# One core, RWKV-6 attention and a squared-ReLU projection: a new written order of all engines, transfers and banks

## The chip, the core and the metric

The kernel runs on one core of a Trainium2 chip. The metric is the device time of one execution in microseconds. Before the change it is 180.9 us, the median of three runs (180.63 to 181.43).

## The reference

Two parts follow each other. The first is a linear attention with a decaying state, for 4 batches of 8 heads, 768 positions and 48 channels; the second is a projection to 2048 channels, a squared ReLU and a projection back to 384.

```python
for t in range(S):
    kt, vt, rt, wt = (k[:, :, t].copy(), v[:, :, t].copy(), r[:, :, t].copy(), w[:, :, t].copy())
    cur = np.einsum('bhd,bhe->bhde', u[None] * kt, vt)
    y[:, :, t] = np.einsum('bhd,bhde->bhe', rt, state + cur)
    state = wt[:, :, :, None] * state + np.einsum('bhd,bhe->bhde', kt, vt)
...
h = x @ w_in
r = np.maximum(h, 0.0)
g = r * r
return (g @ w_out).astype(np.float32)
```

## The kernel before, in words

The work is cut into 12 steps, three for each batch, of 256 positions (two chunks of 128). All steps are unrolled, and there is no loop on the chip. For step s the program has small operations, written as words like `rd_.9.0`: a name, the step, and an index.

- **Loads.** `ld.s.w`, `ld.s.k`, `ld.s.r` and `ld.s.v` (`load_step`, L178) fetch 384 KB each; `ld.g.i` and `ld.g.o` fetch a quarter of a weight matrix (768 KB, L188 and L194), and `cast` (L200) makes it bf16. All are issued by SP, one after the other, in the order of the list, together with the transposing transfers and the stores.
- **Decays.** `ww_` multiplies neighbouring decays (L264), `lw_` takes the logarithm on ScalarE, `cum_` sums it with matmuls (L324 to L328), `exp_` (L340) brings it back. `kw_` and `rw_` (L290, L286) fold a decay into k and r. `rd_.s.1` and `rd_.s.0` (L361, L358, VectorE) write the decayed keys and queries to `kdec_buf` and `rdec_buf`.
- **Attention.** For steps 0 to 3, TensorE transposes these (`tr_`, L374) and `rkt_` copies them to `kT` and `rT` (L391, L389). For steps 4 to 11 a transposing transfer does both (`dtr_`, L401 and L398). `p_` (L418) multiplies them in tiles of 64 rows, `pm_` masks (L432, L429), `su_` (L444, 64 rows) sums the new state, `ts_` and `sn_` (L454, L459) carry it on, `y_` (L481, 128 rows) and `yc_` (L491, 64 rows) make the output. The bonus of the position itself goes through `ku_`, `qp_`, `q_`, `qs_` and `vq_` (L297, L302, L307, L277, L316), and `ysb_` (L502) adds it.
- **Projection.** `yt_` and `xt_` (L514, L519), or from step 6 on a transposing transfer `dyt_` (L523), turn the output into `xT`. `m1_.s.g` (L534) is six matmuls of 128 by 256 into one of four banks, `rl_` (L543 on ScalarE, L545 on VectorE) takes the ReLU out of the bank, `sq_` squares, `m2_.s.c.q` (L562) is four matmuls of 128 by 384, and `os_` (L569, L571) and `store` (L575) bring the result out.
- **Warming.** `warm_.n.i` (L579) is n matmuls of 128 by 512 on zeros; their results are never read. They keep TensorE's clock up while the first loads are on the way.

What sets the order is `ORDER`, a list of 865 such words that was written by a search. The program walks through it once and issues each word as it stands, so that every engine's queue has the words of that engine in the list's order. `=A`, `=V` and `=G` say that ScalarE, VectorE or GpSimd does it, and `:0` and the like name the bank. Each engine works strictly in order: a word that waits holds up all words behind it on its engine. SP's queue is such a queue too.

Of the kernel before, what the change touches and what calls it, by code (L numbers as in the profile page):

```python
# [27 lines left out]
qp_.2=G pm_.2.1 pm_.2.0 su_.2:1 rl_.1.1=V ts_.2.0=V ld.2.i m1_.0.0:2 m1_.1.3:1 cast.i.2=A y_.2:1 q_.2 yc_.2.0
sn_.2.0 yc_.2.1 rl_.1.3=A m1_.0.5:3 ld.3.i m1_.1.5:1 ld.3.w m1_.0.4:0 rl_.0.0=A rl_.0.5=V qs_.2=A rl_.1.5=A
cast.i.3=G m1_.1.7:3 ld.0.o m1_.1.4:1 vq_.2=V ysb_.2=V rl_.0.4=A rl_.1.7=A ww_.3=G cast.o.0=G m1_.0.7:2 yt_.2:3  # L30
ld.2.o m1_.0.6:0 lw_.3 cast.o.2=G cum_.3:1 xt_.2=V rl_.0.7=V ld.3.o m1_.2.4:3 rl_.0.6=V sq_.0.1=A ld.1.o
sq_.0.0=A rl_.1.4=A m1_.2.2:2 sq_.0.2=A m1_.1.6:0 m1_.2.7:1 ld.3.r rl_.1.6=A sq_.1.1=A rl_.2.2=V rl_.2.4=V
# [5 lines left out]
p_.3.1:b ts_.3.0=A m2_.2.0.1:2 m2_.1.0.3 m2_.2.0.3 m2_.1.0.2 sq_.2.0=A ww_.4=G pm_.3.0 lw_.4 q_.3 qs_.3=A
cum_.4:0 m2_.2.0.0 ld.6.w v_.4=A pm_.3.1 ww_.5=G rw_.4=G sn_.3.0 ts_.3.1=V vq_.3=G ac_.4 al_.4 m2_.2.0.2
yc_.3.1:1 y_.3 m2_.2.1.0:1 m2_.2.1.2 os_.1.0=A kw_.4=V lw_.5 ysb_.3=V sn_.3.1 store.0.0 os_.2.0=A exp_.4 kw_.5=G  # L40
rd_.4.1 rd_.4.0 cum_.5:1 ac_.5 yt_.3:3 vs_.4.1=G xt_.3=A ld.5.r vs_.4.0=A al_.5 store.0.1 ld.6.r m2_.2.1.3
m2_.2.1.1 os_.2.1=V m1_.3.0:3 rl_.3.0=A exp_.5 su_.4:0 m1_.3.1:2 rl_.3.1=A m2_.1.1.3:0 m2_.1.1.1 dtr_.4.1
ku_.4=V qp_.4=V rw_.5=V m1_.3.7:2 rl_.3.7=A m1_.3.6:1 ts_.4.0=V dtr_.4.0 rl_.3.6=A m2_.1.1.2 m1_.3.5:3 rd_.5.1
rl_.3.5=A m1_.3.4:1 sn_.4.0 ts_.4.1=V p_.4.0:0 q_.4 rd_.5.0 qs_.4=A ww_.6=G vq_.4=G rw_.6=G p_.4.1:1 sq_.3.0=V
m2_.3.1.0:3 m2_.1.1.0 pm_.4.0 yc_.4.1:0 yc_.4.0 sq_.3.3=A m1_.3.3:2 rl_.3.4=A sq_.3.2=A pm_.4.1 y_.4 lw_.6
m1_.3.2:1 rl_.3.3=A rl_.3.2=A cum_.6:1 m2_.3.0.2:2 m2_.3.0.3 sq_.3.1=A m2_.3.1.3 m2_.3.1.1 ku_.5=G qp_.5=G
ld.5.v ysb_.4=V al_.6 ld.7.w ld.6.k ww_.7=G yt_.4:1 m2_.3.1.2 m2_.3.0.0 exp_.6 ac_.6 os_.1.1=V sn_.4.1 m2_.3.0.1
# [5 lines left out]
m2_.4.1.1:1 xt_.5=A qp_.6=G q_.6 qs_.6=G ld.7.k p_.6.0:1 ld.8.v yc_.6.1:0 ld.7.v ld.8.r p_.6.1:m store.1.1
ld.8.w vq_.6=G ku_.7=G pm_.6.1 sq_.4.3=A kw_.7=G m2_.4.1.0 m2_.4.1.2 m1_.5.1:0 rl_.5.1=A pm_.6.0 m2_.4.1.3
sn_.6.1 m1_.5.0:2 cum_.7:1 y_.6 m1_.5.7:3 vs_.7.0=A rl_.5.0=A os_.4.1=A ww_.9=V al_.7 m2_.4.0.0:0 rl_.5.7=V
m1_.5.2:2 m1_.5.6:1 ww_.8=G rw_.7=G exp_.7 ac_.7 m2_.4.0.1 vs_.7.1=G m2_.4.0.2 m1_.5.3:3 rl_.5.2=A sq_.5.0=A
v_.7=A rl_.5.3=A m1_.5.5:2 sq_.5.1=A ysb_.6=V vs_.8.0=G m2_.4.0.3 lw_.8 rl_.5.6=A rd_.7.1 qp_.7=V rd_.7.0
sq_.5.3=A su_.7:0 v_.8=G rl_.5.5=V rw_.8=V m1_.5.4:3 rl_.5.4=V m2_.5.1.0:2 cum_.8:1 sq_.5.2=A ts_.7.0=V al_.8
q_.7 m2_.5.1.1 m2_.5.1.3 store.1.0 ld.8.k ld.11.k ac_.8 store.3.1 dyt_.6 dtr_.7.1 dtr_.7.0 exp_.8 kw_.8=V
sn_.7.0 ts_.7.1=V m1_.6.2:3 m2_.5.1.2 m1_.6.3:1 ld.9.r ld.10.w sn_.7.1 os_.4.0=A rd_.8.1 m1_.6.1:0 os_.5.1=A  # L60
ku_.8=G m1_.6.7:2 rd_.8.0 rl_.6.2=V ld.9.k rl_.6.3=A qs_.7=A m1_.6.4:1 su_.8:1 rl_.6.7=A p_.7.1:m p_.7.0:0
qp_.8=G rl_.6.1=V ts_.8.0=V yc_.7.1:1 yc_.7.0 rl_.6.4=A sq_.6.1=A m2_.5.0.2:0 m1_.6.6:1 store.3.0 rl_.6.6=A
sq_.6.3=A dtr_.8.1 pm_.7.1 pm_.7.0 lw_.9 dtr_.8.0 m2_.5.0.1 m1_.6.5:2 y_.7 m1_.6.0:3 m2_.5.0.3 m2_.5.0.0
store.4.1 ku_.9=G q_.8 qs_.8=G ww_.10=G rl_.6.5=V vq_.7=V rl_.6.0=A vs_.8.1=A rw_.9=G sq_.6.0=A p_.8.0:m
p_.8.1:0 kw_.9=G qp_.9=G ysb_.7=V cum_.9:1 m2_.6.0.1:1 ld.9.v ld.10.k os_.5.0=A m2_.6.0.3 m2_.6.1.3:0 m2_.6.0.0
sq_.6.2=V m2_.6.0.2 m2_.6.1.0 sn_.8.0 al_.9 exp_.9 pm_.8.0 rd_.9.0 pm_.8.1 dyt_.7 v_.9=A ac_.9 m1_.7.7:2 y_.8:0
# [28 lines left out]
def kernel(  # L95
# [488 lines left out]
    def ld(n, x, h=None):  # L584
# [48 lines left out]
```

## Time and profile before

| what | value |
|---|---|
| median of the timed runs | 180.9 us (180.63 to 181.43) |
| span of the profiled execution | 178.8 us (no other time of this execution is given) |
| median less span | 2.1 us |
| PE (TensorE) busy | 171.0 us, 96% of the span |
| DVE (VectorE) busy | 138.0 us, 77% |
| ACT (ScalarE) busy | 133.4 us, 75% |
| POOL (GpSimd) busy | 108.0 us, 60% |
| transfers | 35.81 MB, mean 200 GB/s |

The span goes from the first to the last instruction of one profiled execution, and all durations below are from that execution. PEld is TensorE's weight load, which overlaps its matmuls. A busy matmul row includes its pipeline, so that rows that follow each other overlap; the distance from one start to the next tells what a matmul costs.

### The profile page before, as it was taken

The numbers are of one execution on the slowest core, as the hardware profiler recorded it, in microseconds if no ns is written. First come the engines' busy times: TensorE is split into PE (matmuls) and PEld (weight loads), VectorE is DVE, ScalarE is ACT, GpSimd is POOL, SyncE is SP. The second block draws the span as 40 slices with busy tenths as digits, with TensorE's granted clock in tenths as the row PEclk, the third lists the DMA queues.
The fourth block names the chain that finished last, engine by engine and source line by source line (L and its number), as shares of the span: only waits on it lengthen the run. The fifth ranks groups of instructions, "written<-read, shape, count | busy, mean of one in ns | idle before, by whom it ended". The sixth has DMA issues, their size and how long they took to land.

```text
span 178.8 us, 5697 instructions
## 1 busy us (share of the span) xinstructions
PE 171.0 (96%) x2383; PEld 123.9 (69%) x2385; DVE 138.0 (77%) x204; ACT 133.4 (75%) x238; POOL 108.0 (60%) x132
## 2 busy tenths in 40 slices
PE   7997889999999999999999999999999999999992
PEld 2354478888776677678677777788866779758761
DVE  5489998678999998998988999886678694705330
ACT  5287969999799768899889979779867528862601
POOL 6539986870784636998499788979997703000000
PEclk9999999999999999999999999999999999999999
DMA  5999999999999799979999998899927471402212
GB/s 144 268 263 252 259 346 361 344 368 260 266 243 237 191 216 185 290 166 259 273 291 151 213 255 224 222 175 245 226 79 148 55 48 40 127 12 88 88 44 88
DMA packets 78952, 35.81 MB, mean 200 GB/s; under 512 B 72144, under 2 KB 77392, under 8 KB 78928
## 3 DMA queue, kind: packets, MB, share of 16 engines
q1 hardware_dynamic: 78928, 35.46, 84.6%
q8 instruction: 18, 0.29, 0.7%
q14 instruction: 6, 0.05, 0.1%
HBM read 25.36 MB, written 4.72 MB: 168 GB/s over the span
## 4 chain that ended last, share of the span: by engine, by line
PE 56%; POOL 16%; DMA 10%; DVE 9%; issue 4%; SPq 3%; ACT 1%; POOLq 0%; ACTq 0%; DVEq 0%
PE m L562 16%; PE bk L534 11%; PE m L534 11%; PE bk L562 10%; DMA k_raw<-in_k_dram 7%; POOL ku L297 3%; DMA kT<-kdec_buf 3%; POOL r_raw L286 2%; SPq L178 2%; POOL ku L302 2%; DVE pmT L432 2%; PE att L418 2%; POOL ku L316 2%; POOL S L459 2%; DVE y_sb L502 2%
## 5 line engine op out<-in xcount | busy, mean ns | idle before, releaser
L534 PEld LDWEIGHTS <-wi_sb 128*128 128x128 bf16 x576 | 54.9, 98 | 10.7 <-ACT wi_sb L200 0.6
L562 PEld LDWEIGHTS <-gt 128*128 128x128 bf16 x384 | 36.7, 98 | 20.6
L534 PE MATMUL m<-xT,wi_sb 128*128 128x256 bf16 x306 | 40.2, 273 | 0.1
L551 ACT ACTIVATE gt<-gt 128x1024 bf16<-128x1024 f16 x37 | 38.1, 1051 | 0.5
L534 PE MATMUL bk<-xT,wi_sb 128*128 128x256 bf16 x270 | 35.8, 273 | 0.4 <-ACT wi_sb L200 0.4
L562 PE MATMUL bk<-wo_sb,gt 128*128 128x384 bf16 x192 | 35.6, 326 | 0.0
L562 PE MATMUL m<-wo_sb,gt 128*128 128x384 bf16 x192 | 35.0, 326 | 0.0
L543 ACT ACTIVATE gt<-m 128x512 f16<-128x512 f32 x33 | 19.4, 595 | 11.5 <-PE m L534 11.2
L543 ACT ACTIVATE gt<-bk 128x512 f16<-128x512 f32 x35 | 20.6, 596 | 7.2 <-PE bk L534 6.9
L545 DVE TENSOR_SCALAR gt<-m 128x512 f16<-128x512 f32 x18 | 12.3, 688 | 13.1 <-PE m L534 12.4
L432 DVE TENSOR_TENSOR pmT<-att,mask 128x1024 bf16<-128x1024 f32 x16 | 19.1, 1218 | 1.9 <-PE att L418 1.8
L316 POOL TENSOR_TENSOR ku<-v_sh,qs 128x768 f32<-128x768 bf16 x9 | 13.3, 1475 | 10.6 <-ACT qs L277 10.5
L459 POOL TENSOR_TENSOR S<-t_state,ac_buf 128x192 bf16<-128x192 f32 x20 | 12.2, 610 | 8.2 <-DVE t_state L454 5.5
L297 POOL TENSOR_TENSOR ku<-k_raw,u_bc 128x768 f32<-128x768 f32 x9 | 16.7, 1854 | 0.2 <-DMA k_raw<-in_k_dram 0.2
L502 DVE TENSOR_TENSOR y_sb<-att,ku 128x768 bf16<-128x768 f32 x12 | 11.5, 955 | 4.4 <-POOL ku L316 2.0
L290 POOL TENSOR_TENSOR k_raw<-k_raw,w_raw 128x384 f32<-128x384 f32 x8 | 8.1, 1012 | 10.9 <-DMA k_raw<-in_k_dram 10.9
L361 DVE TENSOR_TENSOR kdec_buf<-k_raw,att 128x768 bf16<-128x768 f32 x12 | 11.4, 950 | 3.7 <-ACT att L340 3.7
L277 ACT CAST v_sh<-v_raw 64x384 bf16<-64x384 f32 x26 | 13.2, 509 | 0.3
L302 POOL TENSOR_TENSOR ku<-ku,r_raw 128x768 f32<-128x768 f32 x7 | 12.7, 1811 | 0.2
L358 DVE TENSOR_TENSOR rdec_buf<-r_raw,att 128x384 bf16<-128x384 f32 x24 | 12.3, 547 | 0.6 <-POOL r_raw L286 0.4
L277 POOL CAST v_sh<-v_raw 64x384 bf16<-64x384 f32 x18 | 10.0, 556 | 3.3 <-DMA v_raw<-in_v_dram 2.0
L307 DVE TENSOR_REDUCE q<-ku 128x16 f32<-128x768 f32 x12 | 11.3, 944 | 0.0
(99 smaller groups left out, 250.6 us busy)
## 6 DMA issues: line engine op xcount, KB each, us to landing
w_raw<-in_w_dram SPq DMA_DIRECT2D x12, 384.0 KB, 5.7
k_raw<-in_k_dram SPq DMA_DIRECT2D x12, 384.0 KB, 6.2
r_raw<-in_r_dram SPq DMA_DIRECT2D x12, 384.0 KB, 5.6
v_raw<-in_v_dram SPq DMA_DIRECT2D x12, 384.0 KB, 6.7
out_dram<-o_sb SPq DMA_DIRECT2D x24, 192.0 KB, 4.2
w_st<-in_moe_w_in_dram SPq DMA_DIRECT2D x4, 768.0 KB, 8.9
w_st<-in_moe_w_out_dram SPq DMA_DIRECT2D x4, 768.0 KB, 8.3
u_bc<-in_u_dram SPq DMA_DIRECT2D x1, 192.0 KB, 5.0
```

What stands on the lines that cost most here:

```text
L277: copy(out[j * Q:(j + 1) * Q, c], src[c * Q:(c + 1) * Q, :, j])
L297: tensor_mul("ku_", s, h)(tiles["ku", s][:, hs], raw["k", s][:, hs, 1:3, :], u_bc[:, hs, None, :].to_broadcast([C, n, 2, D]))
L302: tensor_mul("qp_", s, h)(ku, ku, raw["r", s][:, heads(h), 0:2, :])
L316: tensor_mul("vq_", s)(vq[:], tiles["vs", s][:], tiles["qs", s][:, :, :, None].to_broadcast([C, 2, H, D]))
L358: nc.vector.tensor_mul(rdec[0][:, ps, j, :, 0:D], x[:, :, j, :].rearrange("p (a e) d -> p a e d", e=2), dec.rearrange("p (a e) d -> p a e ...
L432: nc.vector.tensor_mul(pmT, ps_p[:].rearrange("p e (x t) -> p (e x) t", t=C), mk.to_broadcast([C, 8, C]))
L459: nc.gpsimd.tensor_mul(t[:], tiles.pop(("ts", s, c))[:].rearrange("p (a d) -> p a d", a=HP), tiles["a_c", s][:, :, c, None].to_broadcast([ ...
L502: nc.vector.tensor_add(tiles["ysb", s][:, x].rearrange("p c (a e d) -> p (c a) e d", e=2, d=D), tiles["y", s][:, :, cols].rearrange("p e ( ...
L534: nc.tensor.matmul(ps1[:, j, :], wi_sb[:, n // 4, kk, n % 4 * 128:(n % 4 + 1) * 128], tiles["xT", s][:, :, kk, :], start=(kk == 0), stop=( ...
L543: nc.scalar.activation(rl, m1, AF.Relu, scale=RS)
L551: nc.scalar.activation(gt, rl, AF.Square)
L562: nc.tensor.matmul(m2, gt[:, 4 * q + n, c * C:(c + 1) * C], wo_sb[:, 4 * q + n, :], start=(summed[s, c] == 1 and n == 0), stop=(summed[s, ...
```

## The change

`ORDER` is written anew, again by a search, whose own picture of the machine now lets the fetching of instructions hold up the stream of loads. The list has 865 words as before, and the same ones, but for the warming, which is again nine words and 46 matmuls in other portions. Nearly every word stands elsewhere, 115 of them name another engine, and banks are handed out anew. `warm_` takes a third number that it doesn't use. Line numbers of functions are four lower after the change.

```diff
-ld.0.w ld.0.k ld.0.r ld.0.u ld.1.w ww_.0=V lw_.0 warm_.11.5 cum_.0:0 kw_.0=G exp_.0 rd_.0.1 ld.0.v warm_.8.5
+ld.0.w warm_.2.2.5 ld.0.k ld.0.r warm_.11.2.0 ld.0.u ld.1.w ww_.0=V ld.0.v lw_.0 ld.1.k kw_.0=V cum_.0:1 warm_.8.2.1
...
-    def warm_(n, i):
+    def warm_(n, i, x=0):
```

Ahead of `cum_.0`, TensorE had 11 warming matmuls; now it has 13 (2 and 11). Ahead of the first projection (`m1_`), both lists hold the same attention words on TensorE: steps 0 and 1 up to their outputs, the decays and the transposes of step 2. Counted along TensorE's queue, words of 64 rows (`p_`, `su_`, `yc_`) came in 25 unbroken runs, of which 20 stand behind the first `m1_`; now they come in 24, of which 18 stand behind it (the search counts 23, in its own way).

The first place is VectorE's queue at the program's start, behind the memsets. `ww` is the product of decays, `kdec_buf` and `rdec_buf` the decayed keys and queries, `ku` the bonus, `q` its sum, `rT` the transposed queries. Before:

```order
L264 TENSOR_TENSOR ww<-w_raw 128x384
L361 TENSOR_TENSOR kdec_buf_108<-k_raw,att_86 128x16x48
L358 TENSOR_TENSOR rdec_buf_107<-r_raw,att_86 128x4x2x48 x2
L264 TENSOR_TENSOR ww<-w_raw 128x384
L302 TENSOR_TENSOR ku<-ku,r_raw 128x768
L307 TENSOR_REDUCE q<-ku 128x16
```

And now:

```order
L260 TENSOR_TENSOR ww<-w_raw 128x384
L286 TENSOR_TENSOR k_raw<-k_raw,w_raw 128x8x48
L357 TENSOR_TENSOR kdec_buf_108<-k_raw,att_87 128x16x48
L354 TENSOR_TENSOR rdec_buf_107<-r_raw,att_87 128x4x2x48 x2
L293 TENSOR_TENSOR ku<-k_raw,u_bc 128x768
L385 COPY rT<-m_0_90 128x1024
L298 TENSOR_TENSOR ku<-ku,r_raw 128x768
```

VectorE takes over `kw_.0` (L286), the first product of the bonus (L293) and a copy of step 0's `rT` (L385); it gives `ww_.1` to GpSimd, the copy of step 1's `rT` to ScalarE, and `q_.0` moves back behind the masks.

The second place is SP's queue from the 10th load of k on. `xT` is a transposing transfer for the projection (step 7, and at the other end step 8), `rT` and `kT` those of step 9's queries and keys, `out_0_dram` a store. Before:

```order
L178 DMA v_raw_2392<-in_v_dram 128x8x96
L178 DMA k_raw_2394<-in_k_dram 128x8x96
L523 DMA_TRANSPOSE xT_2429<-y_sb_2381 128x6x128
L178 DMA v_raw_2532<-in_v_dram 128x8x96
L575 DMA out_0_dram<-o_sb_2142 128x384
L178 DMA w_raw_2592<-in_w_dram 128x8x96
L398 DMA_TRANSPOSE rT_2594<-rdec_buf1_109 128x8x128
L178 DMA r_raw_2603<-in_r_dram 128x8x96
L523 DMA_TRANSPOSE xT_2605<-y_sb_2536 128x6x128
L401 DMA_TRANSPOSE kT_2621<-kdec_buf1_110 128x8x128
```

And now:

```order
L174 DMA k_raw_2279<-in_k_dram 128x8x96
L571 DMA out_0_dram<-o_sb_2013 128x384
L519 DMA_TRANSPOSE xT_2371<-y_sb_2334 128x6x128
L174 DMA k_raw_2392<-in_k_dram 128x8x96
L174 DMA w_raw_2401<-in_w_dram 128x8x96
L397 DMA_TRANSPOSE kT_2445<-kdec_buf1_110 128x8x128
L174 DMA r_raw_2520<-in_r_dram 128x8x96
L394 DMA_TRANSPOSE rT_2529<-rdec_buf1_109 128x8x128
L174 DMA v_raw_2553<-in_v_dram 128x8x96
L519 DMA_TRANSPOSE xT_2559<-y_sb_2518 128x6x128
```

The load of step 10's v and the transfer of step 8's `xT` have moved behind step 9's two transposes. Of everything from the program's start, one load, one store and one `xT` fewer stand ahead of the later of these two.

More of the change, by code (lines that the diff above doesn't have):

```diff
@@ L28 @@
[L28 to L32, printed above, removed]
@@ L38 @@
[L38 to L42, printed above, removed]
@@ L43 @@
[L43 to L47, printed above, removed]
@@ L53 @@
[L53 to L57, printed above, removed]
@@ L58 @@
[L58 to L66, printed above, removed]
-yc_.8.1 rd_.9.1 su_.9:1 vs_.9.1=A yc_.8.0 rl_.7.7=A m1_.7.4:3 ld.10.v vq_.8=G ysb_.8=V m1_.7.0:2 lw_.10
@@ new lines @@
+rl_.4.2=A yc_.5.1 su_.6:0 ysb_.5=V m1_.4.3:2 ld.8.v ww_.7=G m1_.4.1:1 ku_.7=V ld.8.k rl_.4.3=A yt_.5:3 qs_.6=G
+m1_.4.6:0 xt_.5=A ld.8.r m1_.4.0:2 rl_.4.6=V rl_.4.1=A m1_.5.0:3 lw_.7 ts_.6.0=V sq_.4.3=V sq_.4.1=A store.1.1 sn_.6.0
+m1_.5.1:0 rl_.5.0=V m2_.4.1.2:1 v_.7=G rl_.4.0=A ts_.6.1=V ww_.8=V rl_.5.1=A p_.6.0:1 kw_.7=G p_.6.1:m sq_.4.0=A
+yc_.6.1:0 pm_.6.0 m2_.4.1.1 ld.9.w lw_.8 ld.9.v m2_.4.1.3 vq_.6=G pm_.6.1 v_.8=A m1_.5.5:0 sq_.5.0=A m1_.5.4:2 qp_.7=V
+vs_.7.0=G cum_.7:1 rl_.5.5=A y_.6 al_.7 m1_.5.3:3 ysb_.6=V exp_.7 m1_.5.2:0 ku_.8=G rl_.5.4=V dyt_.6 m2_.4.1.0
```

105 lines of the change are left out of this document (63 added, 42 removed).

## The prediction

> **What bounds the kernel now.** I began with the page: busy time, the slices, and the chain that ended last.
>
> ```profile
> span 178.8 us, 5697 instructions
> PE 171.0 (96%) x2383; PEld 123.9 (69%) x2385; DVE 138.0 (77%) x204; ACT 133.4 (75%) x238; POOL 108.0 (60%) x132
> ...
> DMA  5999999999999799979999998899927471402212
> ...
> PE 56%; POOL 16%; DMA 10%; DVE 9%; issue 4%; SPq 3%; ACT 1%; POOLq 0%; ACTq 0%; DVEq 0%
> ```
>
> TensorE (PE) is busy for 96%, and the transfers run at 9 tenths for 130 us. The next view splits the span where the first projection starts and where the last one ends; that start and that end follow, from TensorE's timeline and from the chain.
>
> ```profile
> 0.00:26.00 26.00, 21.98 (x324) 12.14 (x326) 20.53 (x36) 17.41 (x36) 19.30 (x30) 1.00 1.02 253
> 26.00:175.40 149.40, 148.98 (x2059) 111.71 (x2059) 117.45 (x169) 115.53 (x202) 88.68 (x103) 1.00 0.84 194
> 175.40:178.80 3.40, 0.01 (x1) 0.00 (x0) 0.00 (x0) 0.49 (x1) 0.00 (x0) 1.00 0.18 64
> ```
>
> ```profile
> 26.02 0.83 PE L534 MATMUL bk<-xT,wi_sb 128*128 128x256 bf16 x6 [0.39 <-ACT wi_sb L200]
> ```
>
> ```profile
> 37.37 0.66 PE m L534 x6
> ...
> 43.20 1.30 PE m L562 x8
> ...
> 173.46 1.96 PE bk L562 x12
> 175.50 0.49 ACT o_sb L569
> ```
>
> The first column behind the stretch is its length, the second PE's busy time. From 26.0 to 175.4 us PE is idle for 149.40 - 148.98 = 0.42 us, and a word of the projections follows the one before it every 0.65 us (0.66 for six of L534, 1.30 for two words of L562). So the time is made of three pieces: a head of 26.0 us until the first `m1_`, 149.4 us in which PE hardly waits, and 3.4 us behind it for the last copy and store. Busy PE time is not always work at full rate; what waits remain shows where the weight loads wait, in the waits of that engine from 26 us on (total, times, longest):
>
> ```profile
> PEld L418 <- issue: 1.4, 5, 0.3
> PEld L444 <- issue: 1.3, 5, 0.3
> PEld L491 <- issue: 0.8, 3, 0.3
> PEld L534 <- ACT wi_sb L200: 0.6, 1, 0.6
> PEld L491 <- DVE pmT L432: 0.5, 2, 0.3
> PEld L418 <- DMA kT<-kdec_buf: 0.4, 1, 0.4
> PEld L418 <- DVE kT L391: 0.3, 1, 0.3
> ```
>
> Those for named engines add up to 0.6 + 0.5 + 0.4 + 0.3 = 1.8 us. That is the most that a better order could take out of the middle; the three "issue" rows (13 waits, 3.5 us, so 0.27 each) stand in front of words of 64 rows.
>
> **The change, part by part.** The words are the same, so PE's work is the same. Ahead of the first `m1_` both lists put the same attention words on PE. What can differ is when the first `m1_` starts, how often PE changes between 64 and 128 rows behind it, and where PE waits. The median of 180.9 is 2.1 us over the profiled span of 178.8; I work on the span and add 2.1.
>
> *The head.* The rows are PE's timeline, then ScalarE's, GpSimd's and VectorE's at the program's start.
>
> ```profile
> 1.19 4.87 PE L579 MATMUL att<-warm 128*128 128x512 bf16 x11 [1.19 <-DVE half_ones L228]
> 5.86 0.28 PE L324 MATMUL att<-half_ones,lw_buf 128*128 128x2 bf16 x4
> ...
> 6.57 1.89 PE L579 MATMUL att<-warm 128*128 128x512 bf16 x8
> ```
>
> ```profile
> 6.78 0.80 ACT L340 ACTIVATE att<-att 128x768 f32<-128x768 f32 x1 [0.97 <-PE att L328]
> ...
> 24.50 1.47 ACT L200 CAST wi_sb<-w_st 128x1536 bf16<-128x1536 f32 x1 [1.57 <-DMA w_st<-in_moe_w_in_dram]
> ```
>
> ```profile
> 7.59 1.00 POOL L286 TENSOR_TENSOR r_raw<-r_raw,w_raw 128x384 f32<-128x384 f32 x1 [0.34 <-DMA r_raw<-in_r_dram]
> ```
>
> ```profile
> 7.66 0.95 DVE L361 TENSOR_TENSOR kdec_buf<-k_raw,att 128x768 bf16<-128x768 f32 x1 [2.47 <-ACT att L340]
> ...
> 9.99 0.80 DVE L264 TENSOR_TENSOR ww<-w_raw 128x384 f32<-128x384 f32 x1 [0.45 <-DMA w_raw<-in_w_dram]
> 10.71 0.95 DVE L302 TENSOR_TENSOR ku<-ku,r_raw 128x768 f32<-128x768 f32 x1
> ...
> 18.22 0.68 DVE L389 COPY rT<-bk 128x1024 bf16<-128x1024 bf16 x1
> ...
> 24.93 0.55 DVE L519 COPY xT<-bk 128x768 bf16<-128x768 bf16 x1
> ```
>
> Eleven warming matmuls take from 1.19 to 5.86, 0.42 each, and the decay sum `cum_.0` (L324) starts as they end. The order has 13 there now. Two more cost 0.85 at this rate, or 0.47 at that of the eight later ones (1.89 / 8 = 0.24). `cum_.0` moves by 0.5 to 0.85, and with it the exponential at 6.78 and VectorE's start at 7.66. A page of the Trainium skill, "TensorE: Matmul & The Clock Gate" (section "Part 1: The HAM clock gate (the "warmup" mystery)"), says that the array runs at half rate until about 3.4 us of activity have gone by; by it the two would come after the release and cost the smaller figure. The trace has the slow rate for at least 4.7 us, so the rows decide here.
>
> From 7.66 to 25.48 (24.93 + 0.55) VectorE (DVE) has one long wait, 0.45 at `ww_.1`, which is GpSimd's now; in its place stands a product that waits for nothing new. In the same stretch it gains the bonus product (0.95, as L302 of that shape) and step 0's copy (0.68), and loses `ww_.1` (0.80) and step 1's copy (0.68): +0.15. So `xT` of step 0 is later by (0.5 to 0.85) - 0.45 + 0.15 = 0.2 to 0.55 us, at 25.7 to 26.0. The first `m1_` needs also its weights' cast, which ends at 24.50 + 1.47 = 25.97 since the load lands then; the same bytes are queued ahead of this load as before, so I leave it there. The later start of the two is thus 26.0, and the transposes that PE does just ahead of it can add some tenths: +0.2, with 0 and +0.85 (nothing absorbed) as ends.
>
> *Changes between 64 and 128 rows.* Behind the first `m1_` there are 18 runs of 64-row words instead of 20. Their price is between 0.1 us (a word of `m1_` takes 0.76 instead of 0.66 behind a run, in the rows below) and twice that with the wait of 0.27 in front: 0.1 to 0.37 for a run. I take 0.2: -0.4 (-0.2 to -0.7).
>
> ```profile
> 33.62 0.37 PE att L491 x32
> 33.99 0.76 PE m L534 x6
> ```
>
> *Waits that go.* The 0.42 us of idle PE belong to the old order: -0.4 (0 to -1.8, the sum of the weight loads' waits above).
>
> *Waits that come.* PE reaches the attention of late steps earlier. Six words of the projections that stood ahead of `p_.9.0` stand behind it now (two of L562, four of L534): 6 x 0.65 = 3.9 us. Before, this word waited for its transposed keys, as the chain shows, and the transfers around it moved this:
>
> ```profile
> 119.72 5.12 DMA kT<-kdec_buf
> 124.88 0.65 PE att L418 x32
> ```
>
> ```profile
> 110.00:120.00 10.00, 10.00 (x179) 7.37 (x179) 8.89 (x15) 7.91 (x15) 8.68 (x12) 1.00 0.97 179
> 120.00:130.00 10.00, 9.78 (x166) 7.99 (x164) 7.12 (x11) 9.02 (x16) 9.45 (x10) 1.00 1.14 240
> ```
>
> The keys landed at 124.84, so the margin was nil. PE now wants them at 124.88 - 3.9 - 0.4 (runs) - 0.4 (idle) + 0.2 (head) = 120.4. Ahead of the later of step 9's two transposes stand one load (0.39 MB), one store and one `xT` (0.20 MB each) fewer: 0.79 MB at 240 GB/s (the last column) is 3.3 us, so they land at 121.5 if the stream is as dense as before. That is 1.1 us late. Where the old queue stood still while SP waited (179 GB/s from 110 to 120 against 240 after it: a quarter of 10 us), the stream can be up to 2.5 us earlier, and nobody waits. Between 0 and +1.1 I take the middle, +0.6. `xT` of step 8 comes just behind in SP's queue, and an `m1_` just behind on PE; its lateness is the same one, not a second. On SP, everything behind a transpose that waits for VectorE waits too, and that is where a further delay would come from.
>
> The fetches of instructions, which the search took into account, are in the page as a queue of their own:
>
> ```profile
> q8 instruction: 18, 0.29, 0.7%
> ```
>
> 0.7% of 16 engines' 178.8 us is 20 us, or 1.1 us of one transfer engine for each of the 18. A transfer spread over 16 engines lands with its slowest, so each fetch may hold up the stream by up to 1.1 us; I cannot see where they fall now, and this is why the term above isn't nil. The Trainium skill's page "Runtime: NRT & Kernel Launch" (section "Instruction fetch mechanics") speaks against planning for them: it calls the cost of crossing a 16 KiB block mostly hidden. By it the term of +0.6 would shrink to nothing, and the sum would be 180.3.
>
> *The end.* PE's last word is an `m2_` in both lists, behind it one copy and one store: 3.4 us as before, since the store of the other half is issued during PE's last words. The other engines are busy for 60 to 77% of the span, and the 115 words that changed hands go in all directions: I cost this at nothing, under the cover of PE's 96%; without it, it would show as waits in the middle, which the term above holds.
>
> Sum: 178.8 + 0.2 - 0.4 - 0.4 + 0.6 = 178.8; with 2.1 it is 180.9. For the few tenths between terms I see no sign.
>
> **The rivals.** *No wait at all (faster).* If the transfers come in time, the list runs PE without a pause behind the head. Then 180.9 - 0.6 (the term of waits that come) leaves 180.3, and if half of the weight loads' other waits (1.8 - 0.4) go too, 179.6. For it: only 0.42 us were idle before, so a list can do it. Against: that leaves no more than about 1.3 us to gain in all, and PE reaches its late words earlier than before with the same transfers.
>
> *The stream is late at step 9 (slower).* Place: `p_.9.0`, whose transposes must land by 120.4. If a fetch or a waiting transpose holds SP's queue for another 1.1 us on top of the 1.1 late above, PE stands for 2.2 us, and since PE has no slack behind it, all of it stays: 180.9 - 0.6 + 2.2 = 182.5. It decides from a landing at 121.9 on (1.5 late, 181.8). For it: the slices of the transfers at 9 tenths until 130 us, and a margin of nil at this very word. Against: the old queue had quiet stretches.
>
> *The head in full (slower).* If VectorE absorbs nothing of the 0.85 and the keys are 1.1 late as well, 180.9 + 0.65 + 0.5 = 182.0. That the new order does not reach the engines is no rival: their queues differ as shown.
>
> **How the numbers follow.** A difference of 0.5% (0.9 us) is about what a measurement of this kernel can tell from none; the three runs before lie within 0.8 us. My forecast, no change at 180.9, has 0.5. No wait at all ends below 180.0 in its further half, and I give what lies there 0.22. The late stream has 0.2 and the full head 0.08, both above 181.8. So: faster 0.22, the same 0.50, slower 0.28. Leaving 0.1 out at each side, the range goes from 179.7 (near the end of the first rival) to 182.7 (just over the second).
>
> **What would show it.** In the profile after: the first L530 row of PE between 25.9 and 26.6 us (the head); PE's idle time from there to its last product under 1.5 us; "issue" waits of 64-row words fewer by about two; at step 9's first L414 word a wait for a transposing transfer of 0 to 1.1 us; 3.4 us behind the last product. I'm wrong if PE has several waits of over 0.5 us behind the head, for loads or for GpSimd (then the order hangs on something that I took as covered), or if the first projection starts before 25.5 us (then the head had a slack that I did not see).

## The result and the profile after

The changed kernel takes 189.75 us (median of four runs, 188.5 to 191.08), the old one on the same chip 181.09: the ratio is 1.0485, 95% interval [1.043, 1.0541]. The forecast was no change, 179.7 to 182.7. The kernel is slower, and the time lies far above the range and above each of the rivals, of which the highest was 182.5. All ratios below are against runs of the old kernel on the same chip in the same batch (medians 180.25 to 181.39). A ratio leaves out runs that took over 1.5% longer than the fastest of their kernel; the medians count every run.

The page of the changed kernel, the lines that answer to those of before, and the granted clock, which was 9 in every slice before:

```profile
span 189.3 us, 5690 instructions
...
PE 174.3 (92%) x2382; PEld 126.3 (67%) x2385; DVE 144.5 (76%) x207; ACT 129.3 (68%) x230; POOL 113.7 (60%) x138
...
PEclk9999957999999999999999999999999999999999
DMA  6999899999996149999999999999949124000214
...
PE 58%; DVE 16%; DMA 10%; POOL 8%; issue 3%; ACT 2%; SPq 1%; DVEq 0%; POOLq 0%; ACTq 0%
```

The operations are the same, yet VectorE is busy for 6.5 us more and GpSimd for 5.7 us more (ScalarE for 4.1 us less). An estimate tells longer instructions from words that changed hands: if every instruction of the two profiles is charged at a short duration of its own form (the tenth percentile), what goes beyond that grows from 6.6 to 12.7 us on VectorE and from 7.3 to 12.6 on GpSimd, and hardly on ScalarE (3.0 to 3.2). So nearly the whole increase is instructions that took longer. TensorE's clock is halved in the sixth slice and lowered in the seventh, and the transfers have a hole in the 13th to 15th. VectorE's share of the chain has grown from 9 to 16%. The same three pieces as before, from the first `m1_` to the last product:

```profile
0.00:28.43 28.43, 22.93 (x323) 13.62 (x327) 22.70 (x37) 18.22 (x37) 19.46 (x29) 0.92 1.02 260
28.43:185.90 157.47, 151.32 (x2061) 112.71 (x2059) 121.80 (x171) 110.59 (x192) 94.19 (x109) 0.99 0.80 176
185.90:189.30 3.40, 0.08 (x1) 0.00 (x0) 0.00 (x0) 0.49 (x1) 0.00 (x0) 1.00 0.52 186
```

The head is 28.43 - 26.02 = 2.41 us longer, the middle 157.47 - 149.40 = 8.07, and the tail has not changed: together the 10.5 us between the spans. The profiled execution is the one of 191.08 us, so this is 1.8 us more than lies between the medians. Of the middle's 8.07, TensorE's idle time makes 6.15 - 0.42 = 5.73 (157.47 - 151.32 against 149.40 - 148.98); the other 2.34 is counted as busy, being matmuls at the half clock or behind a late weight load.

**The head.** TensorE's timeline, with two places where it stands still just before the projections, and the first `m1_`:

```profile
22.60 0.24 PE L320 MATMUL att<-half_ones,lw_buf 128*128 128x2 bf16 x4 [1.74 <-DVE pmT L428]
...
24.66 0.42 PE L487 MATMUL att<-S,rT 64*64 64x48 bf16 x16 [1.48 <-DVE y_sb L498]
...
28.43 1.49 PE L530 MATMUL m<-xT,wi_sb 128*128 128x256 bf16 x6
```

The same stretch in windows of 1 us; the last three columns are the granted clock, the transfers' share and GB/s:

```profile
24.00:25.00 1.00, 0.34 (x16) 0.29 (x15) 1.00 (x2) 0.93 (x6) 0.86 (x1) 0.54 1.03 356
...
30.00:31.00 1.00, 1.00 (x7) 0.74 (x6) 1.00 (x1) 0.00 (x0) 1.00 (x2) 0.55 1.14 319
31.00:32.00 1.00, 1.00 (x40) 0.81 (x39) 0.88 (x2) 0.85 (x2) 1.00 (x1) 1.00 1.30 284
```

A mean of 0.54 between 24 and 25 us and of 0.55 between 30 and 31 puts the half clock at about 24.1 to 30.9 us, 6.8 us long, and from 24.66 on TensorE has all the work there is. Six matmuls of `m1_` follow each other in 1.28 us there (1.49 to the end of the last) instead of 0.66. In the old kernel six warming matmuls stood ahead of `cum_.2` and four behind it, in just these two holes (one of the six has no record):

```profile
19.77 1.24 PE L579 MATMUL bk<-warm 128*128 128x512 bf16 x5 [0.16 <-issue]
...
21.38 1.02 PE L579 MATMUL bk<-warm 128*128 128x512 bf16 x4
```

**The middle.** TensorE's waits from 28 us on (total, times, longest):

```profile
PE m L414 <- ACT gt L539: 1.2, 1, 1.2
PE att L414 <- DMA kT<-kdec_buf: 1.2, 1, 1.2
PE bk L558 <- DVE wo_sb L196: 1.1, 1, 1.1
PE m L558 <- DVE gt L541: 0.7, 1, 0.7
PE m L510 <- DVE y_sb L498: 0.5, 1, 0.5
```

Four of these are the several waits of over 0.5 us that the prediction named as what would prove it wrong, though it named loads and GpSimd, and the rows name ScalarE, VectorE and a transposing transfer. They stand, in order of the rows, at `p_.9.1`, `p_.6.0`, `m2_.0.1.2`, `m2_.1.0.2` and `yt_.4`. Two causes show behind them. The first is VectorE's timeline ahead of the two `m2_` words:

```profile
44.96 1.82 DVE L549 TENSOR_TENSOR gt<-gt 128x1024 bf16<-128x1024 f16 x1
46.70 2.21 DVE L298 TENSOR_TENSOR ku<-ku,r_raw 128x768 f32<-128x768 f32 x1
48.84 1.17 DVE L282 TENSOR_TENSOR r_raw<-r_raw,w_raw 128x384 f32<-128x384 f32 x1
49.94 1.26 DVE L196 CAST wo_sb<-w_st 128x1536 bf16<-128x1536 f32 x1
```

GpSimd works without a pause beside these four. Before, such a square took 0.69 us, with GpSimd idle until 45.08:

```profile
44.54 0.69 DVE L553 TENSOR_TENSOR gt<-gt 128x1024 bf16<-128x1024 f16 x1
```

The old product of L302, of the second row's shape, took 0.95. The second cause is SP's queue in the changed kernel (start, duration of the issue):

```profile
52.83 2.99 SPq L174 DMA_DIRECT2D k_raw<-in_k_dram  x2
63.25 0.36 SPq L571 DMA_DIRECT2D out_dram<-o_sb  x1
67.78 1.33 SPq L394 DMA_TRANSPOSE rT<-rdec_buf  x1
...
70.53 0.58 SPq L174 DMA_DIRECT2D w_raw<-in_w_dram  x1
```

`store.0.0` waits from 55.82 to 63.25 for ScalarE's copy, the transpose behind it until 67.78 for VectorE, and three loads that wait for nothing stand behind both. That is the hole in the transfers. TensorE is busy all the while; the price comes later. The chain of waits runs through the load and through the engines behind it to a word of TensorE:

```profile
70.53 5.47 DMA w_raw<-in_w_dram
...
79.58 0.97 DVE y_sb L498
80.59 0.51 PE m L510 x6
```

### The profile page after: what moved, and what is told of

It reads as the page before. It is cut to its first block, busy times and chain, and to the rows that moved or that the text cites. A ratio compares the mean times of both kernels' runs of the same rounds, so it can differ in the third digit from the quotient of the medians.

```text
span 189.3 us, 5690 instructions
## 1 busy us (share of the span) xinstructions
PE 174.3 (92%) x2382; PEld 126.3 (67%) x2385; DVE 144.5 (76%) x207; ACT 129.3 (68%) x230; POOL 113.7 (60%) x138
## 4 chain that ended last, share of the span: by engine, by line
PE 58%; DVE 16%; DMA 10%; POOL 8%; issue 3%; ACT 2%; SPq 1%; DVEq 0%; POOLq 0%; ACTq 0%
PE m L558 15%; PE bk L530 11%; PE bk L558 9%; PE m L530 9%; DMA w_raw<-in_w_dram 6%; DMA kT<-kdec_buf 3%; PE m L575 3%; DVE ku L298 2%; DVE rdec_buf L354 2%; POOL ku L293 2%; PE att L414 2%; DVE y_sb L498 2%; DVE gt L549 2%; PE att L477 2%; POOL ww L260 1%
## 5 line engine op out<-in xcount | busy, mean ns | idle before, releaser
L558 PEld LDWEIGHTS <-gt 128*128 128x128 bf16 x384 | 36.2, 98 | 22.2 <-issue 2.4
L530 PE MATMUL bk<-xT,wi_sb 128*128 128x256 bf16 x300 | 40.2, 276 | 0.7 <-DVE xT L515 0.3
L530 PE MATMUL m<-xT,wi_sb 128*128 128x256 bf16 x276 | 37.0, 276 | 0.0
L547 ACT ACTIVATE gt<-gt 128x1024 bf16<-128x1024 f16 x33 | 34.3, 1053 | 0.2
L539 ACT ACTIVATE gt<-m 128x512 f16<-128x512 f32 x36 | 21.0, 596 | 10.1 <-PE m L530 9.8
L549 DVE TENSOR_TENSOR gt<-gt 128x1024 bf16<-128x1024 f16 x15 | 13.4, 895 | 3.8 <-ACT gt L539 3.8
L293 POOL TENSOR_TENSOR ku<-k_raw,u_bc 128x768 f32<-128x768 f32 x8 | 15.1, 1892 | 0.4 <-DMA k_raw<-in_k_dram 0.3
L541 DVE TENSOR_SCALAR gt<-bk 128x512 f16<-128x512 f32 x17 | 11.6, 684 | 3.1 <-PE bk L530 3.1
L286 POOL TENSOR_TENSOR k_raw<-k_raw,w_raw 128x384 f32<-128x384 f32 x10 | 11.3, 1128 | 2.9 <-DMA w_raw<-in_w_dram 2.3
L336 ACT ACTIVATE att<-att 128x768 f32<-128x768 f32 x12 | 9.6, 801 | 4.0 <-PE att L324 1.7
L273 POOL CAST v_sh<-v_raw 64x384 bf16<-64x384 f32 x20 | 11.7, 584 | 0.8
```

What stands on the lines that cost most here:

```text
L273: copy(out[j * Q:(j + 1) * Q, c], src[c * Q:(c + 1) * Q, :, j])
L293: tensor_mul("ku_", s, h)(tiles["ku", s][:, hs], raw["k", s][:, hs, 1:3, :], u_bc[:, hs, None, :].to_broadcast([C, n, 2, D]))
L530: nc.tensor.matmul(ps1[:, j, :], wi_sb[:, n // 4, kk, n % 4 * 128:(n % 4 + 1) * 128], tiles["xT", s][:, :, kk, :], start=(kk == 0), stop=( ...
L539: nc.scalar.activation(rl, m1, AF.Relu, scale=RS)
L547: nc.scalar.activation(gt, rl, AF.Square)
L549: nc.vector.tensor_mul(gt, rl, rl)
```

## The experiments

My theory was that three things add up: the clock that falls in the two holes, VectorE and GpSimd slowing each other, and SP's queue standing still. The rival was that one of them carries it all, the others following from it.

| kernel | median us | ratio to the old kernel, 95% interval |
|---|---|---|
| changed | 189.75 | 1.0485 [1.043, 1.0541] |
| `head_before` | 185.44 | 1.0254 [1.0186, 1.0322] |
| `head_after` | 183.36 | 1.0153 [1.0109, 1.0198] |
| `fill` | 185.06 | 1.0278 [1.0206, 1.0351] |
| `sq_act` | 188.46 | 1.0372 [1.0302, 1.0443] |
| `cold_before` | 181.71 | 1.008 [1.0044, 1.0115] |
| `fill_loads` | 184.47 | 1.0189 [1.01, 1.0278] |
| `fill_loads_r` | 183.61 | 1.0149 [1.0079, 1.0219] |
| `mended` | 183.79 | 1.0173 [1.0095, 1.0252] |
| `mended_head` | 182.96 | 1.0142 [1.0065, 1.022] |
| `loads_r` | 186.09 | 1.0215 [1.0158, 1.0272] |
| `warm13` | 180.87 | 0.9994 [0.9967, 1.002] |

**Head and rest apart.** `head_before` has the old order, engines and warming up to the first projection, and the new order from there on; `head_after` is the reverse, with three banks renamed.

```diff
 head_before: words ahead of the first m1_ as in the old order, the rest as in the new
 head_after:  words ahead of the first m1_ as in the new order, the rest as in the old
+yt_.0:1 tr_.2.1:2 tr_.2.0:0
```

> The words that the new list has ahead of its first projection, in the old list's order, on its engines and with its warming; behind them the new list unchanged. In the profile after, TensorE's last product stands 12.1 us behind the sum of its products with the old head: 2.4 us of that when the first projection starts, 1.2 us more because its first two words run at half clock, 8.5 us in waits behind. Theory 'the head alone': the later waits follow from the late head, so nearly all goes, 181 to 182 us. Theory 'each part its own': the head's 3.6 us go and the later waits stay, 185.5 to 186.5 us. Rival 'the head does not matter': the later waits are set by the transfers, and take up what the head gives back, 189 us.

> The reverse: the words that the old list has ahead of its first projection, in the new order, on the new engines and with the new warming (three of them in other banks than the new list gives them, so that no bank is taken while it is in use); behind them the old list unchanged. Theory 'each part its own': 181 + 3.6 = 184.5 us, give or take 0.7, with a clock that falls to half near 24 us. Theory 'the head alone': over 187 us. Rival 'the head does not matter': 181 us.

Either part alone is slower than the old kernel, by 2.5% and by 1.5%; together they would be 4.1%, and the whole is 4.85%. So head and rest each carry a part, the rest the larger. `head_before` ends at the lower edge of what was expected of two separate parts (185.5 to 186.5), `head_after` 0.4 us under it (183.8 to 185.2). In the profile of `head_before` the clock stays full and the first `m1_` starts at 26.49, yet the middle takes 154.59 us, 5.2 more than the old one's: that much of the 8.07 is there without the new head.

**The two holes.** `fill` is the new order with 28 matmuls of 256 columns on zeros, into columns that nothing reads, in the two places.

```diff
-p_.1.0:1 ld.2.v
+p_.1.0:1 fill_.15 ld.2.v
...
-cum_.2:1 kw_.2=G
+cum_.2:1 fill_.13 kw_.2=G
```

> The new list with 28 more matmuls of 128 by 256 on zeros, in columns of a bank that nothing else uses then: 15 behind the product of step 1's keys and queries, where TensorE idled from 20.9 to 22.6 us, and 13 behind the decay sum of step 2, where it idled from 23.2 to 24.7. Theory 'clock': the granted clock stays at 1.0 from 24 to 31 us, the first two projection words follow each other in 0.66 us instead of 1.28, and the first starts near 27.2 instead of 28.4: 1.5 to 2.5 us less, 187.3 to 188.3 us, if the later waits do not take it up. Rival 'the clock falls whatever the idle time': 189.7 us and the same half clock.

The median falls by 4.7 us, the ratio by 2.1 points, and the two intervals are apart. That is more than I expected. Its clock and its first `m1_`:

```profile
PEclk9999999999999999999999999999999999999999
```

```profile
25.58 0.83 PE L530 MATMUL m<-xT,wi_sb 128*128 128x256 bf16 x6
```

The projections start 28.43 - 25.58 = 2.85 us earlier, ahead of the old kernel's 26.02. Not all of that is the holes: the warming at the program's start took 4.29 us in this execution and 5.73 in the profile of the changed kernel (see the end). `fill_loads`, of which below, has the holes filled and as slow a start (its `cum_.0` at 6.63, that of the changed kernel at 6.70), and its first `m1_` starts at 26.72; so at the same start the holes account for 1.7 us. A second effect shows too. GpSimd's casts at 42.9 to 48.1 us, which had stood beside VectorE's products without a pause, now wait for their loads, since the engines come there earlier and the loads do not; VectorE runs alone in the gaps, and the waits at the two `m2_` words (1.1 and 0.7 us) are gone from the list of waits. So in the changed kernel the late head had set the two engines against each other.

`cold_before` puts the question to the old kernel, where it takes the ten matmuls out of the two holes and changes nothing else.

```diff
-p_.1.0:m warm_.6.1 vq_.0=G
+p_.1.0:m vq_.0=G
...
-vs_.1.1=A pm_.1.0 qs_.1=A exp_.2 warm_.4.1 su_.1:m
+vs_.1.1=A pm_.1.0 qs_.1=A exp_.2 su_.1:m
```

> The old order without its two late warming words, the six matmuls behind p_.1.0 and the four behind cum_.2; all else as it was, so about 10 x 0.24 = 2.4 us of TensorE work that nobody needs are left out and TensorE stands still there instead. Theory (the new order lost part of its time since TensorE stood still in these two places and its clock was then lowered): PEclk falls to about half at 23 to 25 us and stays there for some 6 us, and the time goes up by 1.5 to 4 us, to 182 to 184.5. Rival (the clock costs nothing that other waits do not hide; the kernel that filled the two holes gained by a changed hand-over): PEclk may fall, the time stays within 0.5 us of the old kernel's 180.6.

It is slower by 0.8%, 1.4 us, though it does less: just under the theory's range, and clear of the rival's. The granted clock in its windows:

```profile
22.00:23.00 1.00, 0.60 (x32) 0.58 (x32) 1.00 (x3) 0.99 (x3) 1.00 (x2) 0.61 1.00 346
...
25.00:26.00 1.00, 1.00 (x25) 0.77 (x24) 0.74 (x3) 0.80 (x2) 0.81 (x2) 0.69 1.06 311
26.00:27.00 1.00, 1.00 (x14) 0.94 (x14) 0.90 (x2) 1.00 (x3) 0.33 (x1) 1.00 1.07 328
```

By the means of 0.61 and 0.69, the half clock lasts here from about 22.2 to 25.6, 3.4 us, half as long as in the changed kernel. Its ten runs fall into two groups: six with a mean clock of 0.990 or 0.991 (180.85 to 182.0 us) and four with 0.978 to 0.981 (182.07 to 182.97). A clock of 0.99 over 179 us is 3.6 us at half rate, 0.98 twice that. All four runs of the changed kernel have 0.980 to 0.982. So in the old order the clock is worth about 1 us for one such stretch and 2.3 for two (medians of the groups, 181.3 and 182.6, against 180.25). Two of the thirteen runs of the unchanged old kernel have a clock of 0.99 too, and take 181.36 and 181.38 us. If two stretches cost as much in the new order, some 2.4 of the 4.7 us that `fill` won have other reasons; the second effect above is one, and no run isolates it.

**VectorE beside GpSimd.** `probe` is the old kernel with a tail whose results are not kept: squares and products on VectorE alone, then the same beside GpSimd.

```diff
+for _ in range(8): nc.vector.tensor_mul(gt, rl, rl)
+for _ in range(8): nc.vector.tensor_mul(r_[:, :, 2, :], r_[:, :, 1, :], w_[:, :, 0, :])
+nc.vector.tensor_mul(w_[:, :, 1, :], w_[:, :, 0, :], w_[:, :, 0, :])
+(the two loops again)
+for _ in range(30): nc.gpsimd.tensor_mul(k_[:, :, 0, :], k_[:, :, 1, :], w_[:, :, 1, :])
```

> The old order, with a tail that computes nothing that is kept: on VectorE eight squares of sq_'s form and eight products of rw_'s form alone, one product on which GpSimd's start hangs, and the same sixteen again, while GpSimd does thirty products of kw_'s form, the last of them alone. Theory (VectorE and GpSimd slow each other): the squares take 0.7 us alone and 1.2 to 2.2 beside GpSimd, the products 0.5 to 0.6 alone and 0.9 to 1.3 beside it; GpSimd's products take 0.6 to 1.0 alone and 1.2 to 2 beside VectorE. Rival (in the new order they were stretched by something else, by transfers or by ScalarE): each kind takes the same in both stretches, within 0.1 us.

VectorE's timeline (the second column is the time of all eight), then GpSimd's windows beside VectorE's squares, beside its products and alone:

```profile
174.77 5.78 DVE L586 TENSOR_TENSOR gt<-gt 128x1024 bf16<-128x1024 f16 x8 [0.74 <-PE bk L559]
180.46 4.70 DVE L588 TENSOR_TENSOR r_raw<-r_raw,w_raw 128x384 f32<-128x384 f32 x8
...
185.54 10.51 DVE L591 TENSOR_TENSOR gt<-gt 128x1024 bf16<-128x1024 f16 x8
195.98 10.24 DVE L593 TENSOR_TENSOR r_raw<-r_raw,w_raw 128x384 f32<-128x384 f32 x8
```

```profile
185.70:196.00 10.30, 9.74 (x8) 0.50 0.00 0
196.00:206.20 10.20, 9.57 (x9) 0.50 0.00 1
206.20:222.00 15.80, 14.70 (x15) 0.50 0.00 0
```

A square costs 5.78 / 8 = 0.72 us alone and 1.31 beside GpSimd; a product 0.59 and 1.28. GpSimd's products follow each other every 1.07 us alone, every 1.40 beside squares and every 1.27 beside products, in step with VectorE's. The theory holds, and hardly a transfer ran here to take the blame. Two instructions of the head show what it does in the kernel. The changed kernel, GpSimd's product and VectorE's:

```profile
10.14 1.00 POOL L260 TENSOR_TENSOR ww<-w_raw 128x384 f32<-128x384 f32 x1 [1.52 <-DMA w_raw<-in_w_dram]
```

```profile
10.27 1.69 DVE L293 TENSOR_TENSOR ku<-k_raw,u_bc 128x768 f32<-128x768 f32 x1
```

And `fill_loads_r`, of which below:

```profile
9.85 0.95 DVE L294 TENSOR_TENSOR ku<-k_raw,u_bc 128x768 f32<-128x768 f32 x1
```

```profile
9.97 1.69 POOL L261 TENSOR_TENSOR ww<-w_raw 128x384 f32<-128x384 f32 x1 [1.39 <-DMA w_raw<-in_w_dram]
```

In both, the one that starts first takes its usual time and the other one waits. The Trainium skill's page "SBUF — State Buffer" (section "SBUF: two separate sides") states this as a rule: a VectorE operation with two inputs in SBUF and a GpSimd operation that reads SBUF take a shared pair of ports as a lock, and the later one is blocked. These four rows agree. The probe agrees in direction, but a pair took (10.51 - 0.72) / 7 = 1.40 us (the first square ran ahead of GpSimd's start) where the two alone add up to 0.72 + 1.07 = 1.79, so a part of each still overlaps.

`sq_act` moves four squares from VectorE to ScalarE in the new order.

```diff
-sq_.0.1=V sq_.0.2=V sq_.1.1=V sq_.1.2=V
+sq_.0.1=A sq_.0.2=A sq_.1.1=A sq_.1.2=A
```

> The new list with four squares of steps 0 and 1 (words sq_.0.1, sq_.0.2, sq_.1.1, sq_.1.2) on ScalarE instead of VectorE, as the old list has three of them. Theory 'contention': on VectorE two of these took 1.8 us each instead of 0.69 while GpSimd was busy, and with other stretched words they made the cast of the second weights late (it ended at 51.2 us), for which TensorE waited 1.4 us, and 1.0 us just behind: both waits go, about 2 us less, 187.5 to 188 us. Rival 'ScalarE becomes the bound there': no gain, 189 to 190 us, with waits for ScalarE's copies in the place of the cast's.

VectorE's busy time falls from 144.5 to 139.7 us, 4.8 for four squares that are worth 4 x 0.69 = 2.8 alone, and the two waits at `m2_` go. But TensorE now waits 1.3 us for ScalarE's logarithm at `cum_.3`, and the interval meets that of the changed kernel: for the time, inconclusive.

**SP's queue.** `fill_loads` is `fill` with three loads ahead of the store and the store behind step 4's transposes; `fill_loads_r` moves one more load.

```diff
-ld.6.k ... store.0.0 ... dtr_.4.0 ... dtr_.4.1 ... ld.6.w ... ld.6.r ... ld.7.w
+ld.6.k ld.6.w ld.6.r ld.7.w ... dtr_.4.0 ... dtr_.4.1 store.0.0
...
-dyt_.7 ... ld.11.k ... ld.11.w ... dtr_.9.1 ... ld.10.r
+ld.10.r dyt_.7 ... ld.11.k ... ld.11.w ... dtr_.9.1
```

> The new order with the two holes of TensorE filled, and on SP the loads of step 6's w and r and of step 7's w ahead of store.0.0, the store behind step 4's transposes. Queue theory (the store that waits for ScalarE at 55.8 to 63.3 us, and the transposes behind it, hold the loads back until 70.5, and the transposes of step 6 are late by it): the transfers no longer stand still at 61 to 70 us, the first product of step 6 (p_.6.0) loses its wait of 1.1 us, and the time goes from 185.1 to 183.5 to 184.3. Rival (engines that hand over late decide, not the queue): 184.8 or more, with the wait of 1.1 us still there or moved to another word of steps 5 to 7.

> As the kernel with the three loads ahead of the store, and in addition the load of step 10's r ahead of the transposing transfer of step 7's output, three transfers earlier than it was. Queue theory: VectorE's product with that load at 128 us no longer waits, the waits of TensorE at p_.9.1 and yc_.9.1 (1.2 and 0.5 us) go, and the time is 1.2 to 1.8 us below that of the kernel without this move, 182 to 183. Rival (the two engines that slow each other there, VectorE's product taking 1.75 us beside GpSimd, decide): at most 0.5 us below.

The two together take `fill` from 1.0278 to 1.0149; each step alone is within the intervals, and even those of the whole still touch. Both medians lie between what the queue theory and its rival had said. The transfers still slow down: from 61 to 66 us they move 103 GB/s in `fill_loads` (86 in `fill`), since SP then waits for step 4's transposes. The profiles of TensorE are clearer: the wait for `kT` at `p_.6.0` is gone in both, and in the second `p_.9.1` no longer waits for ScalarE. In their place stands another transfer that is now late, that of `xT` at `m1_.7.5` (1.1 us).

The profile of `fill_loads` (a run of 186.41 us) shows one thing more. Its clock is full, but its start is slow, and the two waits at the `m2_` words are back (1.0 and 0.7 us). The first `m1_`, and the product of L298 that meets GpSimd again:

```profile
26.72 0.82 PE L530 MATMUL m<-xT,wi_sb 128*128 128x256 bf16 x6
```

```profile
43.04 2.21 DVE L298 TENSOR_TENSOR ku<-ku,r_raw 128x768 f32<-128x768 f32 x1
```

So these waits do not need the half clock; a head that is 1.1 us later than that of `fill` is enough here (the loads that were moved are issued only from 55.11 us on, behind these waits). VectorE's stretch of the same place in `fill_loads_r`, whose first `m1_` starts at 25.94, and GpSimd's cast that waits:

```profile
41.26 0.68 DVE L550 TENSOR_TENSOR gt<-gt 128x1024 bf16<-128x1024 f16 x1
41.85 0.95 DVE L299 TENSOR_TENSOR ku<-ku,r_raw 128x768 f32<-128x768 f32 x1
42.72 0.55 DVE L283 TENSOR_TENSOR r_raw<-r_raw,w_raw 128x384 f32<-128x384 f32 x1
```

```profile
44.01 1.47 POOL L197 CAST wo_sb<-w_st 128x1536 bf16<-128x1536 f32 x1 [2.88 <-DMA w_st<-in_moe_w_out_dram]
```

The same three instructions that took 1.82 + 2.21 + 1.17 us beside GpSimd take 0.68 + 0.95 + 0.55 here. `loads_r` has the moves on SP alone, without the filled holes.

> The new order as it is, the two holes of TensorE not filled, with only the moves on SP: step 6's w and r and step 7's w ahead of store.0.0, the store behind step 4's transposes, and step 10's r ahead of the transposing transfer of step 7's output. Queue theory (these waits are costs of their own, whatever the clock does in the head): the waits at p_.6.0, p_.9.1 and yc_.9.1 (1.2, 1.4 and 0.5 us) go, one of up to 1.3 us comes at m1_.7.5, and the ratio to the old kernel falls from 1.0485 to 1.03 to 1.038. Rival (they only showed what the late head had cost anyhow, or other waits take their place): 1.043 or more.

The ratio is 1.0215, lower than the theory had said; the median of all six runs, 186.09, is 2.9% over the old kernel. Either way the moves win: each of the six (183.41 to 187.58) is below each of the changed kernel's four (188.5 to 191.08). The profile is of a run of 187.56 us and still has the waits at the two `m2_` words (1.1 and 0.7 us), while those at `p_.6.0` and `p_.9.1` are gone; the one that was expected at `m1_.7.5` did not come.

Filling the holes alone wins 2.1 points and moving the loads alone 2.7 (2.0 by all six runs), but both together win 3.4, not 4.8 (4.1). They may share a part, as they would if a late head and late loads make the same engines meet; the intervals do not settle it. Neither edit wins back the whole, so the rival that one cause carries it all does not hold for these two. How much VectorE and GpSimd carry by themselves no timed run isolates.

**What is left.** `mended` puts the load of step 10's r behind `dyt_.7` and gives one square to ScalarE; `mended_head` also has 11 warming matmuls again and the old engines for two products of the head.

```diff
-sq_.1.2=V ... ld.10.r dyt_.7
+sq_.1.2=A ... dyt_.7 ld.10.r
...
-warm_.2.2.5 ... ku_.0=V ... ww_.1=G
+ku_.0=G ... ww_.1=V
```

> As the kernel with the two holes filled, the three loads ahead of the store and the early load of step 10's r, with two more edits: that load stands one place later, behind the transposing transfer of step 7's output instead of ahead of it, and one square (sq_.1.2) is ScalarE's, which stood idle there, instead of VectorE's, where it took 1.8 us beside GpSimd and held up step 2's copy of xT. Theory (a hand-over that VectorE and GpSimd stretch, and a transfer that stands behind another, each cost TensorE their own wait): the waits of 1.27 us at m1_.7.5 and of 0.49 at m1_.2.2 go, the time is 1 to 1.8 us below the 183.6 before these two edits, 181.8 to 182.6. Rival (some other hand-over is next late by about as much, since no engine has room): within 0.5 us of 183.6.

> As the mended kernel, and at the program's start two warming matmuls fewer (11 ahead of cum_.0, as in the old order) and ku_.0 on GpSimd and ww_.1 on VectorE, as in the old order. Theory (the two more cost up to 0.85 us where the clock is released late, and VectorE's product beside GpSimd's another 0.7): the decay sum starts at 5.7 to 5.9 in every execution instead of 5.7 to 6.7, the runs lie closer together and the time is 0.5 to 1 us below the mended kernel's, near 181. Rival (the first projection waits for its weights' cast or for the transposes in any case): within 0.3 us of the mended kernel.

The rival holds for `mended`: the waits at `m1_.7.5` and `m1_.2.2` went as expected, but `cum_.3` and `p_.9.0` wait instead, and the time is the same. `mended_head` is 0.8 us lower by the medians, within the intervals. None of the kernels beats the old one. The middle of `mended_head`, and the wait at `p_.9.0`:

```profile
25.63:177.40 151.77, 149.91 (x2062) 112.00 (x2059) 117.30 (x171) 111.37 (x194) 93.83 (x110) 1.00 0.82 189
```

```profile
122.39 0.43 PE L414 MATMUL att<-rT,kT 64*64 64x128 bf16 x16 [0.58 <-DMA rT<-rdec_buf]
```

The head is as good as the old one's (25.63), the middle still 151.77 - 149.40 = 2.37 us longer: 1.44 of idle time (1.86 against 0.42) in waits of at most 0.6 us, and 0.93 counted as busy. Whether these many small waits have the same causes was not tried, so what carries the last 1.4 to 1.7% stays open.

`warm13` tests one term of the prediction in the old kernel.

```diff
-warm_.11.5
+warm_.13.5
```

> The old order with 13 warming matmuls ahead of cum_.0 instead of 11, and nothing else changed. Theory of the prediction (VectorE and the cast absorb most): 0.2 us, at most 0.85, slower; the decay sum starts 0.5 to 0.85 us later. Rival (where the old head has no slack and the clock is released late, the whole of it stays): 0.5 to 0.9 us slower.

0.9994 [0.9967, 1.002]: two more warming matmuls cost nothing that can be measured in the old order. (In the profiled execution the thirteen took 4.69 us and `cum_.0` started at 5.81, no later than the 5.86 of before.)

## Why the prediction was wrong

- **What bounds the kernel** was read rightly for the old order, wrongly for the new one. "149.4 us in which PE hardly waits" is a property of the old order, and not of the work. I let the middle start from there and asked only what one word would wait for. It came out at 157.47.
- **The head, +0.2 (0 to +0.85); measured +2.41 to the first `m1_`, and more behind it.** The failing step is "Ahead of the first `m1_` both lists put the same attention words on PE". That is true of the attention words and leaves out the warming words between them. The old profile shows warming around `cum_.2`, the new order has none there, and I costed only the two that moved to the front. Those cost nothing measurable in the old order (`warm13`). In the profile of the changed kernel their shift is there, at the upper end that I gave: `cum_.0` starts at 6.70 instead of 5.86, VectorE's first decayed keys at 8.47 instead of 7.66. The removed ones cost 0.8% in the old order (`cold_before`) and, with what follows from them, 2.1 points in the new one (`fill`).
- **"A product that waits for nothing new"** took 1.69 us instead of the 0.95 that I charged, since GpSimd's product, which was VectorE's before, ran beside it. So VectorE absorbed nothing: `xT` of step 0 starts at 26.51 instead of 24.93.
- **Fewer changes between 64 and 128 rows, -0.4.** Not confirmed. I expected two fewer issue waits; the rows of 64-row words count 8, 3 and 4 (L414, L440, L487) where the old ones had 5, 5 and 3. No experiment isolates this term.
- **Waits that go, -0.4.** They went, and 6.15 us of other idle time came.
- **Waits that come, +0.6 at step 9.** The mechanism was right and the place was one of many. In the changed kernel `p_.9.0` starts at 129.97 and does not wait for its transposes, as TensorE is late itself by then. In `mended_head`, where most of that lateness is gone, it waits 0.58 us, the size that I had given; SP's queue is another one there, so the equal size is in part luck.
- **"The 115 words that changed hands go in all directions: I cost this at nothing, under the cover of PE's 96%."** By its size this is the step that failed most: the middle grew by 8.07 us, 5.73 of them TensorE's idle time. A share of 96% covers nothing if TensorE's own banks wait for VectorE's and ScalarE's copies. I also summed durations of VectorE and GpSimd from a profile in which the two met less (by the estimate above, 6.6 and 7.3 us of lengthening instead of 12.7 and 12.6); they are not constants. I named the price of a lost cover as "waits in the middle" and gave it no number.
- **SP.** I wrote that everything behind a transpose that waits stands too, "and that is where a further delay would come from", and looked for it at step 9 only. It was a store of step 0's output and a transpose of step 4 behind it, 60 us earlier; moving loads ahead of them won 2.0 to 2.7 points (`loads_r`).
- **The tail** was right: 3.4 us.

## What to carry to other kernels

Before costing a reordered program by its busiest engine, walk every place at which that engine will stand still in the new order, and ask what stood there before: a warming matmul may be holding the clock. Where VectorE reads two operands from SBUF while GpSimd works, charge what the pair takes together (here 1.40 us for a square and a product that take 0.72 and 1.07 alone). On a queue that issues in order, look at each store for the loads behind it, and follow them to the words that need them, which came 10 us (`yt_.4`) and 25 us (`p_.6.0`) later here.

## What the runs showed of the hardware

- The half clock lasted 3.4 us in `cold_before` (22.2 to 25.6) and 6.8, twice that, in the changed kernel (24.1 to 30.9), and the mean clocks of single runs fall into 0.99 and 0.98. The Trainium skill's page "TensorE: Matmul & The Clock Gate" (section "Part 1: The HAM clock gate (the "warmup" mystery)") has a free-running window of about 3.4 us; these lengths agree. It also has the clock back after one busy window. In `cold_before` it came back after one, in which TensorE was busy for 3.14 of 3.42 us; in the changed kernel not after the first, in which it stood still until 24.66 and was busy for 2.83 of 3.42, but after the second, busy throughout. That agrees if a window must be busier than 2.83 us to count; where the limit lies no run here shows.
- The pace of the first matmuls changes from one execution to the next. Thirteen warming matmuls took 5.73 us in the profile of the changed kernel and 4.29 in that of `fill`, with the same words. The granted clock reads 1.00 in both there, so that the clock makes this difference is not shown:

```profile
1.19 5.73 PE L575 MATMUL m<-warm 128*128 128x512 bf16 x13 [1.19 <-DVE half_ones L224]
```

```profile
1.19 4.29 PE L575 MATMUL m<-warm 128*128 128x512 bf16 x13 [1.19 <-DVE half_ones L224]
```

- Just before `p_.6.0` got its keys at 95.5 us in the changed kernel, the transfers stood still from about 92.3 to 94.2, with loads queued; the one transfer of another kind in this window (91.5 to 95 us) is a fetch of instructions:

```profile
q8 instruction: 1, 0.02, 2.1%
```

  2.1% of 16 engines' 3.5 us is 1.2 us of one engine. That the fetch caused the stop was not tested, so what the Trainium skill's page "Runtime: NRT & Kernel Launch" (section "Instruction fetch mechanics") says, that the cost of crossing a block of instructions is mostly hidden, stays open here.
